# Block attention and feed-forward on one core: the mask rows ahead of the first splits, the weights' scalings behind the first casts, and shorter chains for the last query block

## The chip, the core and the metric

The kernel runs on one core of a Trainium2 chip. The metric is the time of one execution in microseconds (us). The engines named below are TensorE (PE; its weight loads are PEld), VectorE (DVE), ScalarE (ACT) and GpSimd (POOL); SP is the queue that issues the transfers (DMA) of this kernel.

## What is computed

The reference is block-causal attention over 8 batches of 8 heads, 576 positions and head size 64, followed by a feed-forward of two matrix products with a piecewise activation:

```python
scores = (1.0 / np.sqrt(64)) * np.matmul(q, k.transpose(0, 1, 3, 2))   # q, k, v: (8, 8, 576, 64)
mask = (pos[:, None] // 64) >= (pos[None, :] // 64)                    # pos = arange(576)
scores = np.where(mask, scores, -1000000000.0)
attn = np.exp(scores - np.max(scores, axis=-1, keepdims=True))
attn = attn / (np.sum(attn, axis=-1, keepdims=True) + 1e-09)
x = np.matmul(attn, v)              # then to (4608, 512)
h = x @ w_in                        # w_in: (512, 2048)
g = np.where(h >= 1, h, np.where(h <= -1, 0.0, (h + 1) ** 2 / 4))
return g @ w_out                    # w_out: (2048, 512)
```

## The kernel before

All matrix operands are kept as a sum of two parts, a rounded one and the rest, so that TensorE can take them in its fp32r type and the products come out near fp32: xh and xl for x, wih and wil for w_in, and the two halves of wo_split (in device memory) for w_out. `convert` splits 64 pieces of the weights (128x256 each): a load into bits on SP (L160), two scalings on ScalarE (L165, L166), three bit operations on VectorE (L167, L170, L173), an addition on GpSimd (L179), a cast on ScalarE (L181), a subtraction on GpSimd (L183).

Attention runs in 32 pairs of heads, four for each batch. Of a pair, queries and keys are loaded (qn, kn), split on VectorE (`split_q`, L310 and L311; `split_k`, L320 and L321), turned by TensorE through products with the identity (`turned`, L346), and cast on ScalarE into qb and kb (L351); the part that belongs in qa and ka is copied by VectorE for the first head of the first pair (L353) and by a transfer for all others (L357). The scores are two products, qa with ka (L391) and qb with kb (L394). qa and ka have four more partitions than the 64 of a head, which hold the rows that add the mask: they are made once in mrow, out of the selector sel (a tile msel with ones where the partition's number is that of the query tile), and moved into both heads' qa and ka by four transfers on SP (L148, L149). A softmax of a tile of 128 queries takes the negated maximum (L414), an exponential with a sum (L418), an addition of EPS and a reciprocal in `inverse` (L400, L401), and a scaling (L424).

The last blocks of 64 queries of both heads of a pair make one tile of their own in `scores_last`. Its 576 keys don't fit in one bank of PSUM (the matrix engine's result memory), so they come in two halves: two maxima (L438), their minimum after negation (L442), two exponentials with sums (L444), the sum of these (L448), `inverse`, the scaling (L450). After that TensorE turns the scaled rows, in `turn_last` (L463 in the first batches, L461 in the others, where they first move through a transfer, L239 or L246).

`attention_steps` is a generator with eight steps for each pair. The main loop draws after each of them as many weight pieces as are due (24 in the first 36 steps) and, from step 36 on, one step of the feed-forward: for 512 tokens, w_in (L646), the activation (L655 to L661), w_out (L670, L675). A scheduler sets each engine's order: the text of the program gives an instruction's place among equals, but it may move up when its inputs and slots are expected to be ready. `tc.issue_after(x)` keeps the instructions of the block behind x on x's engine. Tiles come from pools of few slots: a tile gets a slot when an earlier tile in it has been read for the last time. ident_f, mtmp and msel, and the bits of every second weight piece among the first 32, share the two slots of the tag t; the work tiles of those pieces share two slots of the tag gl.

## Time and profile before

| | |
|---|---|
| time, median of 3 runs | 1271.27 us (1271.11 to 1272.6) |
| the profiled execution | 1272.09 us, span of its instructions 1270.3 us |
| PE (matmuls) busy | 1210.7 us, 95% of the span |
| DVE busy | 856.4 us, 67% |
| ACT busy | 701.3 us, 55% |
| POOL busy | 456.3 us, 36% |

The shares are means over stages that differ: attention alone at the start, attention with feed-forward up to about 1075 us, feed-forward alone after that. So the busy times are read by stretches, and the first microseconds instruction by instruction. In the rows below an instruction has its start, its duration, its engine and line, the operation, result<-inputs with shapes, and in brackets how long the engine had been idle before it and what ended that. An instruction that waits inside its own execution shows a longer duration instead. Groups of instructions give a count, the busy time and the mean duration.

### The profile page before, as it was taken

Reading aid. Unit: us, or ns where it says so; the run is one execution under the profiler, and the core shown is the slowest. Engines: PE = TensorE matmul, PEld = TensorE weight load, DVE = VectorE, ACT = ScalarE, POOL = GpSimd, SP = SyncE. Lnnn points to the kernel's source line nnn. Section 1 sums busy time; section 2 is a strip of 40 time slices with the busy share of each in tenths; the row PEclk is TensorE's granted clock in tenths of the full one; section 3 lists DMA queues with packets and bytes.
Section 4 is the critical chain, followed back from the end, with each engine's and each line's share of the span. In section 5 each row is a group of like instructions: output and inputs, shape, how many; then the busy total and the mean of one; then the engine's idle time right before and its main releaser. Section 6 shows DMA issues by size and latency. Waiting matters only on the chain.

```text
span 1270.3 us, 20591 instructions
## 1 busy us (share of the span) xinstructions
PE 1210.7 (95%) x6496; PEld 1018.4 (80%) x6496; DVE 856.4 (67%) x2164; ACT 701.3 (55%) x1827; POOL 456.3 (36%) x454
## 2 busy tenths in 40 slices
PE   5879887899999999999999999999999999999998
PEld 4667666688888888888888888888888888888886
DVE  8998877857776777777777777777777676222222
ACT  5877656546565655566556656555565564222222
POOL 3555655523332333333333333333333332222222
PEclk9888989899999999999999999999999999999999
DMA  5656666655444545564455545454445443322432
GB/s 157 182 165 213 196 228 210 212 184 173 148 152 147 191 144 161 158 193 149 148 162 168 178 141 161 153 181 143 152 154 184 151 132 117 127 92 97 133 100 100
DMA packets 146093, 201.30 MB, mean 158 GB/s; under 512 B 63152, under 2 KB 93872, under 8 KB 145984
## 3 DMA queue, kind: packets, MB, share of 16 engines
q1 hardware_dynamic: 145984, 199.98, 50.4%
q8 instruction: 52, 0.85, 0.3%
q14 instruction: 57, 0.47, 0.1%
HBM read 120.59 MB, written 17.83 MB: 109 GB/s over the span
## 4 chain that ended last, share of the span: by engine, by line
PE 68%; DVE 8%; ACT 4%; issue 3%; DMA 3%; POOL 2%; SPq 0%; ACTq 0%; POOLq 0%; DVEq 0%
PE ph L646 26%; PE po L670 16%; PE po L675 8%; PE ps_av L500 7%; PE ps_t L461 3%; PE ps_s L394 3%; PE ps_s L391 3%; ACT pr L418 2%; PE ps_qk L346 2%; DMA prr<-pr 2%; DVE t L656 2%; DVE nm L414 1%; DVE t L659 1%; DVE pr L424 1%; POOL work L179 1%
## 5 line engine op out<-in xcount | busy, mean ns | idle before, releaser
L661 POOL TENSOR_TENSOR gl<-t,gh 128x512 fp32r<-128x512 f32 x144 | 186.9, 1298 | 604.7 <-ACT gh L660 301.8
L670 PE MATMUL po<-wo,gh 128*128 128x512 f32 x1152 | 296.9, 399 | 0.1
L656 DVE SCALAR_TENSOR_TENSOR t<-t 128x512 f32<-128x512 f32 x144 | 112.9, 784 | 200.2 <-ACT t L655 198.5
L646 PE MATMUL ph<-xh,wih 128*128 128x512 f32 x576 | 237.6, 413 | 2.7 <-DVE t L659 1.8
L670 PEld LDWEIGHTS po<-wo,gh 128*128 128x128 f32 x1152 | 207.7, 188 | 39.3 <-ACT gh L660 0.6
L646 PE MATMUL ph<-xl,wih 128*128 128x512 f32 x576 | 227.4, 395 | 0.9 <-DVE xl L536 0.9
L646 PE MATMUL ph<-xh,wil 128*128 128x512 f32 x576 | 227.4, 395 | 0.0
L655 ACT ACTIVATE t<-ph 128x512 f32<-128x512 f32 x144 | 86.1, 598 | 184.7 <-PE ph L646 184.7
L418 ACT ACTIVATE pr<-ps_s,nm 128x128 f32<-128x128 f32 (+3 forms) x256 | 134.4, 529 | 50.6 <-DVE nm L414 50.3
L414 DVE TENSOR_REDUCE nm<-ps_s 128x1 f32<-128x128 f32 (+3 forms) x256 | 123.6, 485 | 48.7 <-PE ps_s L394 47.4
L675 PE MATMUL po<-wo,gl 128*128 128x512 f32 x576 | 155.3, 391 | 0.0
L660 ACT CAST gh<-t 128x512 fp32r<-128x512 f32 x144 | 89.6, 622 | 102.1 <-DVE t L659 101.7
L391 PE MATMUL ps_s<-ka,qa 68*128 68x288 f32 (+4 forms) x384 | 122.5, 334 | 9.1 <-ACT kb L351 4.2
L646 PEld LDWEIGHTS ph<-xh,wil 128*128 128x128 f32 x576 | 109.1, 189 | 24.1
L675 PEld LDWEIGHTS po<-wo,gl 128*128 128x128 f32 x576 | 108.1, 188 | 23.3
L646 PEld LDWEIGHTS ph<-xh,wih 128*128 128x128 f32 x576 | 109.1, 189 | 21.7 <-DVE t L659 2.4
L646 PEld LDWEIGHTS ph<-xl,wih 128*128 128x128 f32 x576 | 109.6, 190 | 20.2 <-DVE xl L536 1.5
L394 PE MATMUL ps_s<-kb,qb 128*128 128x288 f32 (+4 forms) x384 | 121.4, 323 | 0.0
L454 ACT CAST pb<-ps_t 128x512 fp32r<-128x512 f32 (+1 forms) x120 | 65.5, 546 | 85.6 <-PE ps_t L461 83.8
L424 DVE TENSOR_SCALAR pr<-pr,sm 128x128 f32<-128x128 f32 (+3 forms) x256 | 104.8, 430 | 4.0
L336 POOL TENSOR_TENSOR vsr<-vn,vsr 64x64 fp32r<-64x64 f32 (+1 forms) x96 | 72.8, 768 | 88.6 <-ACT vsr L335 88.6
L456 DVE TENSOR_TENSOR pb<-ps_t,pb 128x512 fp32r<-128x512 f32 (+1 forms) x120 | 75.6, 630 | 40.4 <-ACT pb L454 39.9
(101 smaller groups left out, 1961.4 us busy)
## 6 DMA issues: line engine op xcount, KB each, us to landing
wo<-wo_split SPq DMA_DIRECT2D x144, 512.0 KB, 3.4
prr<-pr SPq DMA_DIRECT2D x96, 192.0 KB, 2.7
prr<-pr SPq DMA_DIRECT2D x72, 256.0 KB, 2.6
out_dram<-ob SPq DMA_DIRECT2D x36, 256.0 KB, 3.9
qn<-in_q_dram SPq DMA_DIRECT2D x32, 256.0 KB, 2.9
kn<-in_k_dram SPq DMA_DIRECT2D x32, 256.0 KB, 2.9
bits<-in_moe_w_in_dram SPq DMA_DIRECT2D x32, 256.0 KB, 3.6
bits<-in_moe_w_out_dram SPq DMA_DIRECT2D x32, 256.0 KB, 3.2
```

The costliest lines, as they stand in the source:

```text
L391: nc.tensor.matmul(ps, qa[:KA, j, c0 : c0 + P], ka[:KA, j, k0 : k0 + n], start=first, stop=False)
L394: nc.tensor.matmul(ps, qb[:, j, c0 : c0 + P], kb[:, j, k0 : k0 + n], start=False, stop=last)
L414: nc.vector.tensor_reduce(out=nm[:, i : i + 1], in_=ps[:, cs], axis=AX.X, op=ALU.max, negate=True)
L418: nc.scalar.activation(pr[:, cs], ps[:, cs], AF.Exp, bias=nm[:, i : i + 1], scale=1.0, accum_out=sm[:, i : i + 1],)
L424: nc.vector.tensor_scalar_mul(pr[:, cs], pr[:, cs], sm[:, i : i + 1])
L500: nc.tensor.matmul(ps[:, lo_col:], vt, x, start=first and i == 0 and m == 0, stop=last and i == len(parts) - 1 and m == len(mov) - 1,)
L646: nc.tensor.matmul(ph, w[:, cc, fs], x[:, cc, xs], start=(cc == 0 and i == 0), stop=(cc == NCC - 1 and i == 2),)
L656: nc.vector.scalar_tensor_tensor(out=t_, in0=t_, scalar=1.0, in1=t_, op0=ALU.min, op1=ALU.mult)
L660: nc.scalar.copy(gh, t_)
L661: nc.gpsimd.tensor_tensor(out=gl, in0=t_, in1=gh.bitcast(F32), op=ALU.subtract)
L670: nc.tensor.matmul(po[tt], gh[:, ts_], wo[:, w, :], start=(fc == 0 and w == 0), stop=False)
L675: nc.tensor.matmul(po[tt], gl[:, ts_], wo[:, 0, :], start=False, stop=fc == NFC - 1)
```

## The change

Four things are changed. msel gets a slot of the tag gl, is filled at the top of the function ahead of the identity, and by GpSimd alone. The zeroing of the last columns of qa and qb moves ahead of the mask rows, the four transfers of the mask rows directly behind them in the text, and both splits of the queries and keys (`split_queries` and `split_keys` hold the old bodies) stay behind the last mask row, by `issue_after(masked)`. The two scalings of a weight piece stay behind the last cast of turned queries of the first pair, by `issue_after(casts[-1])`. In `scores_last` the minimum becomes a tensor_scalar with one half's maximum as its scalar, and sum and EPS are added in one tensor_scalar, so that `inverse` isn't called there.

```diff
@@ -83,6 +83,13 @@
         return ps_w.tile([P, 512], F32, tag="work", name=name)
 
 
+    msel = ffn.tile([P, 512], F32, tag="gl", name="msel")
+    sel = msel[:NTL, : NTL * BLK].rearrange("p (t c) -> p t c", c=BLK)
+    nc.gpsimd.memset(msel[:NTL, : NTL * BLK], 0.0)
+    nc.gpsimd.affine_select(
+        out=sel, in_=sel, compare_op=ALU.not_equal, fill=1.0, base=0,
+        pattern=[[-1, NTL], [0, BLK]], channel_multiplier=1,
+    )
     ident_f = ffn.tile([P, 512], F32, tag="t", name="ident_f")[:, :P]
     make_identity(nc, ident_f)
     ident_r = const.tile([P, P], F32R, tag="ident", name="ident_r")
@@ -118,35 +125,27 @@
     vsr = [const.tile([P, NTL + 1, 2, D], F32R, tag=f"vsr{j}", name=f"vsr{j}") for j in range(2)]
 
     mtmp = ffn.tile([P, 512], F32, tag="t", name="mtmp")
-    msel = ffn.tile([P, 512], F32, tag="t", name="msel")
     nc.vector.memset(mtmp, 0.0)
-    nc.vector.memset(msel[:NTL], 0.0)
-    nc.gpsimd.affine_select(
-        out=msel[:NTL, : NTL * BLK].rearrange("p (t c) -> p t c", c=BLK),
-        in_=msel[:NTL, : NTL * BLK].rearrange("p (t c) -> p t c", c=BLK),
-        compare_op=ALU.not_equal, fill=1.0, base=0,
-        pattern=[[-1, NTL], [0, BLK]], channel_multiplier=1,
-    )
-    sel = msel[:NTL, : NTL * BLK].rearrange("p (t c) -> p t c", c=BLK)
+    for t_ in (qa, qb):
+        nc.vector.tensor_copy(
+            t_[:, :, SM:], mtmp[:, : 2 * (QW - SM)].rearrange("p (h c) -> p h c", h=2)
+        )
     for side in range(2):
         nc.vector.tensor_copy(mrow[:, side, :512], mtmp[:NTL, :512])
         nc.vector.tensor_copy(mrow[:, side, 512:S], mtmp[:NTL, : S - 512])
     rows = mrow[:, :, :SM].rearrange("p s (t c) -> p s t c", c=P)
     nc.vector.tensor_copy(rows[:, 0, :, :BLK], sel)
-    nc.vector.tensor_scalar_mul(rows[:, 1, :, BLK:], sel, MASKED)
-    for t_ in (qa, qb):
-        nc.vector.tensor_copy(
-            t_[:, :, SM:], mtmp[:, : 2 * (QW - SM)].rearrange("p (h c) -> p h c", h=2)
-        )
+    masked = nc.vector.tensor_scalar_mul(rows[:, 1, :, BLK:], sel, MASKED)
+    for j in range(2):
+        nc.sync.dma_start(qa[D:KA, j, :S].bitcast(F32), mrow[:, 0, :].bitcast(F32))
+        nc.sync.dma_start(ka[D:KA, j, :].bitcast(F32), mrow[:, 1, :].bitcast(F32))
     for t_ in pcs:
         nc.vector.tensor_copy(t_[BLK:], mtmp[BLK:, : 2 * BLK].rearrange("p (h c) -> p h c", h=2))
     for t_ in vsr:
         nc.vector.tensor_copy(
             t_[BLK:, NTL, :, :], mtmp[BLK:, : 2 * D].rearrange("p (h c) -> p h c", h=2)
         )
-    for j in range(2):
-        nc.sync.dma_start(qa[D:KA, j, :S].bitcast(F32), mrow[:, 0, :].bitcast(F32))
-        nc.sync.dma_start(ka[D:KA, j, :].bitcast(F32), mrow[:, 1, :].bitcast(F32))
+    casts = []
 
 
     def convert(n, source, hi, lo, done):
@@ -162,8 +161,10 @@
         low = bits[:, :, 0]
 
 
-        nc.scalar.mul(top, bits[:, :, 1].bitcast(F32), 2.0**-112)
-        nc.scalar.mul(low, low.bitcast(U32), 2.0**-29)
+
+        with tc.issue_after(casts[-1].ins):
+            nc.scalar.mul(top, bits[:, :, 1].bitcast(F32), 2.0**-112)
+            nc.scalar.mul(low, low.bitcast(U32), 2.0**-29)
         nc.vector.tensor_scalar(
             out=top, in0=top, scalar1=F32_TOP, scalar2=-F32_TOP, op0=ALU.min, op1=ALU.max
         )
@@ -304,6 +305,10 @@
 
         def split_q(self):
 
+            with tc.issue_after(masked.ins):
+                self.split_queries()
+
+        def split_queries(self):
             qn = self.nat.pop("q")[:, : 2 * NTL + 1, :]
             self.qs = att1.tile([P, 2 * NTL + 1, 2, D], F32R, tag="qs", name="qs")
             for c0, c1 in ((0, 2 * NTL), (2 * NTL, 2 * NTL + 1)):
@@ -314,6 +319,10 @@
             )
 
         def split_k(self):
+            with tc.issue_after(masked.ins):
+                self.split_keys()
+
+        def split_keys(self):
             kn = self.nat.pop("k")[:, : 2 * NTL + 1, :]
             self.ks = att1.tile([P, 2 * NTL + 1, 2, D], F32R, tag="ks", name="ks")
             for c0, c1 in ((0, 2 * NTL), (2 * NTL, 2 * NTL + 1)):
@@ -348,7 +357,9 @@
                 )
 
             turned = ps[:, :SM].rearrange("p (t c) -> p c t", t=NTL)
-            nc.scalar.copy(bt[:, j, :SM].rearrange("p (c t) -> p c t", t=NTL), turned)
+            cast = nc.scalar.copy(bt[:, j, :SM].rearrange("p (c t) -> p c t", t=NTL), turned)
+            if self.first and is_q:
+                casts.append(cast)
             if self.first and j == 0:
                 nc.vector.tensor_copy(
                     a[:D, j, :SM].rearrange("p (c t) -> p c t", t=NTL), turned[hi0 : hi0 + D]
@@ -439,14 +450,19 @@
                     out=nm[:, i : i + 1], in_=ps[:, :half], axis=AX.X, op=ALU.max, negate=True
                 )
                 banks.append(ps)
-            nc.vector.tensor_tensor(out=nm[:, 2:3], in0=nm[:, 0:1], in1=nm[:, 1:2], op=ALU.min)
+            nc.vector.tensor_scalar(
+                out=nm[:, 2:3], in0=nm[:, 0:1], scalar1=nm[:, 1:2], scalar2=None, op0=ALU.min
+            )
             for i in range(2):
                 nc.scalar.activation(
                     pr[:, i * half : (i + 1) * half], banks[i][:, :half], AF.Exp,
                     bias=nm[:, 2:3], scale=1.0, accum_out=sm[:, i : i + 1],
                 )
-            nc.vector.tensor_tensor(out=sm[:, 2:3], in0=sm[:, 0:1], in1=sm[:, 1:2], op=ALU.add)
-            self.inverse(sm[:, 2:3])
+            nc.vector.tensor_scalar(
+                out=sm[:, 2:3], in0=sm[:, 0:1], scalar1=sm[:, 1:2], scalar2=EPS,
+                op0=ALU.add, op1=ALU.add,
+            )
+            nc.vector.reciprocal(sm[:, 2:3], sm[:, 2:3])
             nc.vector.tensor_scalar_mul(pr, pr, sm[:, 2:3])
             self.pr["last"] = as_float32r(pr, self.plain) if self.hop else [pr]
 
```

The scheduler's orders for the two kernels differ on TensorE in about the first 960 matmuls, on the others there above all, and on VectorE also for each pair's last block. On ScalarE at the start of the program, before (L165 and L166 scale the first weight pieces, L351 casts turned queries and keys, L370 the last blocks):

```order
L165 ACT_TABLE_LOAD
L165 ACTIVATE work_202<-bits_201 128x256
L351 CAST qb_103<-ps_qk_150 128x512
L351 CAST kb_105<-ps_qk_157 128x512
L351 CAST qb_103<-ps_qk_164 128x512
L351 CAST kb_105<-ps_qk_187 128x512
L166 ACTIVATE bits_201<-bits_201 128x256
L370 CAST qb_103<-ps_qk_230 128x2x64
L165 ACTIVATE work_241<-bits_240 128x256
```

and with the change (the lines are now L360 for the casts, L166 and L167 for the scalings):

```order
L360 ACT_TABLE_LOAD
L360 CAST qb_108<-ps_qk_150 128x512
L360 CAST kb_110<-ps_qk_157 128x512
L360 CAST qb_108<-ps_qk_164 128x512
L360 CAST kb_110<-ps_qk_187 128x512
L166 ACTIVATE work_202<-bits_201 128x256
L167 ACTIVATE bits_201<-bits_201 128x256
L166 ACTIVATE work_212<-bits_211 128x256
L167 ACTIVATE bits_211<-bits_211 128x256
```

The four casts have gone ahead of the first scaling, and a second scaled piece ahead of the last blocks.

On SP at the start of the program, behind the loads of the first pair, before:

```order
L160 DMA bits_201<-in_moe_w_in_dram 128x512
L160 DMA bits_240<-in_moe_w_in_dram 128x512
L295 DMA qn_306<-in_q_dram 128x2x256
L148 DMA qa_102<-mrow_106 4x576
L149 DMA ka_104<-mrow_106 4x576
```

and with the change (L159 loads weights, L140 and L141 move the mask rows):

```order
L159 DMA bits_201<-in_moe_w_in_dram 128x512
L159 DMA bits_211<-in_moe_w_in_dram 128x512
L159 DMA bits_240<-in_moe_w_in_dram 128x512
L140 DMA qa_107<-mrow_111 4x576
L141 DMA ka_109<-mrow_111 4x576
```

The load of the second pair's queries has gone behind the mask rows, and a third load of weights has come ahead of them.

On VectorE, from behind the minimum of the second pair's last block (L442) to its scaling (L450), with sm_560 the block's sums, before (L167, L170 and L173 belong to weight pieces, L320 to the next pair's keys, L414 to maxima of other tiles):

```order
L170 TENSOR_SCALAR work_602<-work_602 128x256
L320 CAST ks_609<-kn_589 128x8x64
L173 SCALAR_TENSOR_TENSOR work_602<-work_602 128x256
L320 CAST ks_609<-kn_589 128x64
L414 TENSOR_REDUCE nm_615<-ps_s_613 128x1 x2
L448 TENSOR_TENSOR sm_560<-sm_560 128x1
L414 TENSOR_REDUCE nm_644<-ps_s_642 128x1
L400 TENSOR_SCALAR sm_560<-sm_560 128x1
L167 TENSOR_SCALAR work_673<-work_673 128x256
L401 RECIPROCAL sm_560<-sm_560 128x1
L167 TENSOR_SCALAR work_700<-work_700 128x256
L450 TENSOR_SCALAR pr_558<-pr_558,sm_560 128x576
```

and with the change, behind the minimum L453 (sm_559 the block's sums; L461 the sum, L465 the reciprocal, L466 the scaling; L168 and L174 weights, L425 maxima, L435 another tile's scaling):

```order
L435 TENSOR_SCALAR pr_531<-pr_531,sm_533 128x512
L425 TENSOR_REDUCE nm_613<-ps_s_611 128x1 x2
L174 SCALAR_TENSOR_TENSOR work_671<-work_671 128x256
L461 TENSOR_SCALAR sm_559<-sm_559 128x1
L425 TENSOR_REDUCE nm_642<-ps_s_640 128x1
L465 RECIPROCAL sm_559<-sm_559 128x1
L168 TENSOR_SCALAR work_698<-work_698 128x256
L466 TENSOR_SCALAR pr_557<-pr_557,sm_559 128x576
```

Between the sum and the scaling an addition and one bit operation on weights are gone; the keys' split and two bit operations have left the part ahead of the sum, and another tile's scaling has come in.

## Rows read from the trace of the kernel before

**Rows 1.** Busy time by stretches: us from:to, length, busy per engine (count), clock, DMA

```profile
12.00:100.00 88.00, 71.33 (x365) 57.97 (x365) 81.20 (x249) 69.92 (x215) 47.46 (x58) 0.88 0.60 176
...
100.00:300.00 200.00, 178.74 (x895) 142.13 (x895) 151.83 (x384) 123.24 (x345) 99.91 (x117) 0.96 0.65 206
...
300.00:1060.00 760.00, 754.46 (x4307) 647.91 (x4305) 553.13 (x1407) 451.33 (x1169) 259.25 (x233) 1.00 0.51 158
```

**Rows 2.** Timeline, start, DVE: start us, us, engine, line, operation, shapes [idle before <-releaser]

```profile
4.09 0.48 DVE L123 MEMSET msel<- 4x512 f32 x1
...
4.66 1.00 DVE L311 SCALAR_TENSOR_TENSOR qs<-qn,qs 128x576 fp32r<-128x576 f32 x1
...
6.39 0.20 DVE L320 CAST ks<-kn 128x64 fp32r<-128x64 f32 x1 [0.40 <-DMA kn<-in_k_dram]
...
6.62 0.76 DVE L321 TENSOR_TENSOR ks<-kn,ks 128x576 fp32r<-128x576 f32 x1
...
7.64 0.28 DVE L136 TENSOR_SCALAR mrow<-msel 4x256 fp32r<-4x256 f32 x1
```

**Rows 3.** The same timeline: PE, ACT and DVE up to the first scores

```profile
7.58 0.75 PE L346 MATMUL ps_qk<-ident_r,qs 128*128 128x128 f32 x4 [7.58 <-DVE ident_r L89]
...
10.26 0.43 ACT L165 ACTIVATE work<-bits 128x256 f32<-128x256 f32 x1 [8.25 <-DMA bits<-in_moe_w_in_dram]
...
10.72 0.29 DVE L167 TENSOR_SCALAR work<-work 128x256 f32<-128x256 f32 x1 [2.81 <-ACT work L165]
...
11.97 0.69 DVE L353 CAST ka<-ps_qk 64x512 fp32r<-64x512 f32 x1
...
12.02 0.61 ACT L351 CAST kb<-ps_qk 128x512 fp32r<-128x512 f32 x1
...
12.72 0.47 PE L391 MATMUL ps_s<-ka,qa 68*128 68x128 f32 x1 [2.62 <-DVE ka L353]
```

**Rows 4.** The same timeline: issues on the SP queue

```profile
6.66 1.06 SPq L160 DMA_DIRECT2D bits<-in_moe_w_in_dram  x2
...
9.17 0.61 SPq L149 DMA_DIRECT2D ka<-mrow  x1
```

**Rows 5.** DMA issues, 0 to 20 us: count, KB each, us to landing

```profile
qn<-in_q_dram SPq DMA_DIRECT2D x2, 256.0 KB, 3.9
...
kn<-in_k_dram SPq DMA_DIRECT2D x4, 16.0 KB, 2.5
```

**Rows 6.** Timeline, second pair: the last query block on DVE, and PE behind it

```profile
46.40 0.21 DVE L448 TENSOR_TENSOR sm<-sm 128x1 f32<-128x1 f32 x1
...
47.06 1.04 DVE L167 TENSOR_SCALAR work<-work 128x256 f32<-128x256 f32 x1
...
48.75 0.51 DVE L450 TENSOR_SCALAR pr<-pr,sm 128x576 f32<-128x576 f32 x1
...
49.41 1.30 PE L463 MATMUL ps_t<-ident_r,pr 128*128 128x128 f32 x5 [3.78 <-DVE sm L400]
```

**Rows 7.** Waits of PE, 0 to 100 us: us in total, times, longest

```profile
PE ps_t L463 <- DVE sm L400: 7.4, 3, 3.8
```

**Rows 8.** Groups by line, shape: count | busy us, mean ns | idle before

```profile
L400 DVE TENSOR_SCALAR sm<-sm 128x2 f32<-128x2 f32 x64 | 30.6, 478 | 26.1 <-ACT pr L418 26.1
...
L400 DVE TENSOR_SCALAR sm<-sm 128x1 f32<-128x1 f32 x160 | 23.1, 145 | 5.9 <-ACT pr L418 2.6
...
L442 DVE TENSOR_TENSOR nm<-nm 128x1 f32<-128x1 f32 x32 | 13.2, 412 | 0.9
...
L448 DVE TENSOR_TENSOR sm<-sm 128x1 f32<-128x1 f32 x32 | 5.9, 185 | 18.2 <-ACT pr L444 18.2
```

**Rows 9.** Timeline, GpSimd and DVE: a late minimum of a last query block

```profile
149.99 1.42 POOL L321 TENSOR_TENSOR ks<-kn,ks 128x576 fp32r<-128x576 f32 x1 [0.43 <-DVE ks L320]
...
150.31 1.12 DVE L442 TENSOR_TENSOR nm<-nm 128x1 f32<-128x1 f32 x1
```

**Rows 10.** Busy time by stretches, one of ten us

```profile
220.00:230.00 10.00, 7.40 (x19) 5.52 (x20) 8.12 (x25) 6.58 (x20) 4.92 (x6) 0.66 0.77 259
```

## The prediction

> **What bounds the kernel now.** I read the busy time by stretches first [rows 1]. From 300 us on TensorE works 754.5 of 760 us; what other engines save there has nowhere to go. From 12 to 100 us it works 71.3 of 88 and VectorE 81.2; from 100 to 300 us TensorE still idles 21.3 us. So time can be won before the first matmul, and where TensorE waits in the first 300 us. A head start gained there is kept, since the work after it is dense.
>
> The timeline of the start shows two waits. On VectorE the memset of msel stands at 4.09 us, between the splits, because its slot of the pool comes free only when mtmp has been read; the splits end at 7.38 (6.62 + 0.76), then comes the cast of the identity, and the last mask row is written at 7.64 to 7.92 [rows 2]. TensorE's first turn of queries waits for the identity until 7.58. On ScalarE the first weight scaling (L165) waits 8.25 us for its load, until 10.26, and the casts of the turned queries and keys (L351), whose turns were done from 8.3 on, queue behind it. VectorE stands 2.81 us before L167, which takes ScalarE's result; its cast into ka ends at 12.66 and the first scores start at 12.72 [rows 3].
>
> In the second pair the last query block shows the other kind: its sum at 46.40, its scaling at 48.75 to 49.26, and TensorE, whose next work turns that block, stands still for 3.78 us [rows 6]. Three such waits make 7.4 us of the first 100 [rows 7].
>
> **The change part by part: the start.** In the changed order the mask rows and the identity's cast stand ahead of the splits, the memset of msel is on GpSimd. VectorE's work up to the splits' end loses 0.48 (memset) and keeps the rest: ident_r, L135, L136 only change places, some 0.8 us (0.28 for L136, the others alike) going ahead of the query split. That split is then done some 0.6 us later than it was (0.8 less what VectorE had stood idle before it); the key split ends at the same 7.4 us, since it waits for the last piece of kn, landed at 6.39. The query split would end at 5.66 + 0.6, and the query turns start right behind it, at about 6.3 us instead of 7.58 [rows 2]; the key turns start at 7.4 instead of 8.1. All turns are done some 0.7 us earlier.
>
> ScalarE now has the four casts first. Each takes about 0.6 us, as the last of the four in [rows 3]; the first key cast ends near 8.8, the copy into ka near 9.5 instead of 12.66. So the casts are 3 us earlier, but **what is late next** is the mask rows' transfer into qa and ka, which the first scores read. SP is the queue to look at: it issues in order, and the mask rows stand behind two weight loads (1.06 us for both) and one query load and the one into ka is issued from 9.17 to 9.78 [rows 4]. The new order has three weight loads and no query load ahead of them: 256 KB as well, and no more than 0.6 us to issue, so the same place within 0.1 us, and the same issue times. Having the rows ready at 4 us instead of 7.9 thus buys nearly nothing. The ka row then lands, from its issue near 9.2: after 2.5 us if like the 16 KB loads, after 3.9 if like the 256 KB loads of queries [rows 5], so at 11.7 or 13.1; for less there is only that issue starts are 0.6 us apart, so no earlier than 9.8. I take 11.6, nearest to the small loads (9 KB here). The first scores start there instead of at 12.72: 1.1 us earlier, with bounds of 2.9 earlier and 0.4 later.
>
> Of this VectorE has to make use, as it is nearly full from 12 us on. Its 2.81 us in front of L167 stay open up to 10.7, as L165 still waits for its load to land at 10.26 [rows 3]. The two L353 copies (0.7 us each) now fill this gap, but VectorE then waits for the first scores instead. I count **1.0 us** for the start, with bounds of -0.4 and 2.4 (for more than 2.4, VectorE would have to have no idle time at all there).
>
> **The small operations.** Per pair one VectorE instruction goes: sum, add of EPS and reciprocal become two instead of three. The row of the single add is 145 ns [rows 8], the step to the next instruction some 0.2 us by my estimate. In nine pairs up to 300 us that is 1.8 us of VectorE's chain in front of the last block's scaling.
>
> Further, the order of what lies between changes. In the second pair, between the sum (46.40) and the scaling (48.75) there stand two L167 of weights, one of which took 1.04 us; in the new order one of them is left there. TensorE waits for just this chain (3.78 us) [rows 6]. So this wait shrinks by 0.2 (only the add) up to 1.2 us (the long L167 too). The first pair's order loses one L167 from the same place, so the same bounds; for the third to fifth I take 0.2 each. That is 1.0 to 3.0 us for five pairs; moved work has to be done elsewhere on a full VectorE, so I take **2.0**.
>
> The minimum (L442) has a mean of 412 ns for one number per partition; L400 on the same width has 145, on two numbers 478 [rows 8]. One of 1.12 us began and ended inside a subtraction of GpSimd, the end of both being 151.4 [rows 9]. The new form, a tensor_scalar of width one, is that of L400's 145 ns row. From 100 to 300 us such waits are worth 1.0 (rows 9) and at most 32 x 0.04 = 1.3 in L448 (185 ns against 145 [rows 8]); most of L442's others come after 300 us, where TensorE is full. With the 0.8 us of four shorter chains in these 200 us the bounds are 0 and 3.1. I take **0.7**, nearer to nothing, since TensorE is idle there only a tenth of the time [rows 1].
>
> The Trainium skill speaks against this last term at one point. "VectorE: DVE Perf Modes", section on mode 2x_2P, lets a one-source operation in SBUF use both read ports when its outermost non-unit dimension is even, or odd and equal for source and destination, and "SBUF — State Buffer", section "two separate sides", says such an operation and GpSimd shut each other out for a whole instruction. If width one counts as odd and equal, the new minimum would wait as the old one did, this term would be 0.3 instead of 0.7, and the sum 3.3 instead of 3.7 us. The two rows of L400 speak otherwise, 478 ns at width two and 145 at width one [rows 8], so I keep 3.7.
>
> **Rivals.** *The full engine keeps it.* VectorE stays the bound up to 100 us, and only the VectorE time that is gone comes back: 0.48 of memset and five adds, 1.0, together 1.5 us; the shorter waits of TensorE are filled by moved weight work. For it: 81.2 of 88 us [rows 1]. Against it: the 6.8 us in which VectorE stands idle in the same stretch, so it isn't the bound throughout. That gives 1271.3 - 1.5 = 1269.8.
>
> *A new order costs the clock.* TensorE's order differs in about the first 960 matmuls (transposes and scores swap places with the first feed-forward matmuls). Where TensorE has waited, stretches at the lower of its clock levels (1.2 of 2.4 GHz) follow: 220 to 230 us has 7.40 us of work and a granted clock of 0.66 [rows 10], against 1.00 from 300 us on [rows 1]. One further stretch like this costs 0.34 x 10 = 3.4 us if TensorE is the bound behind it. Its place is the stretch from 100 to 300 us; it opens if a wait of TensorE there grows to that of the second pair, 3.78 us. With the first rival's 1.5 us it gives 1271.3 - 1.5 + 3.4 = 1273.2, slower. A stretch avoided, by the same row, would give 1264.2 together with my sum.
>
> *The mask rows don't come earlier.* If they land at 13.1, as a load of 256 KB would, the start loses 0.4 instead of winning 1.0: 3.7 - 1.4 = 2.3 us, 1269.0. For it: three weight loads ahead of them on SP. Against it: 9 KB, and a start at 12.72 that was a cast's doing.
>
> **How the numbers follow.** 1.0 + 2.0 + 0.7 = 3.7 us. The profiled execution took 1272.1 us (span 1270.3), 0.8 above the median of 1271.3: it would take 1268.4, and the median 1267.6. Chances: this sum 0.52, the first rival 0.2, the mask rows' 0.12, the clock rival 0.16. What a measurement here can tell from no change is 0.2%, 2.5 us: faster than 1268.7 or slower than 1273.8. Of the sum's case I count 0.43 as faster and 0.09 (its lower terms) as the same; the first rival and the mask rows' give 0.07 to faster and 0.25 to the same, the clock rival 0.06 to the same and 0.10 to slower. So 0.50 faster, 0.40 same, 0.10 slower. Range: 1264.2 (a clock stretch less) to 1272.9, most of the clock rival's side left out.
>
> **What would show it.** First scores near 11.6 us with the wait in front of them put down to the mask rows' transfer, not to a cast; ScalarE's first four instructions being casts that end near 10 us. The wait of TensorE before the second pair's last block under 3.0 us. The new minimum at about 0.15 us through the whole run. Matmul lines in the dense part unchanged. If the stretches up to 300 us show more time at the lower clock, the second rival is right; if TensorE's idle time up to 100 us stays while VectorE's busy time falls by 1.5 us only, the first.

## The result: 0.24% slower, and the profile after

The changed kernel takes 1274.61 us in the median of 9 runs, beside 1271.27 us of the kernel before on the same chip: ratio 1.0024, 95% interval 1.0014 to 1.0035, so 3.1 us slower (1.8 to 4.4). The forecast was 3.7 us faster. The profiled execution took 1274.26 us (span 1272.5). Further down the kernel before was run anew beside each group of kernels (medians from 1269.8 to 1271.3), and each ratio is to those runs.

Busy time by stretches in the changed kernel, columns as in [rows 1], with two stretches of ten us:

```profile
12.00:100.00 88.00, 71.84 (x381) 58.14 (x382) 79.44 (x249) 70.18 (x217) 48.10 (x60) 0.94 0.61 179
100.00:300.00 200.00, 176.45 (x861) 140.09 (x860) 155.48 (x372) 119.22 (x332) 98.58 (x114) 0.92 0.63 202
300.00:1060.00 760.00, 753.42 (x4305) 646.72 (x4304) 544.52 (x1378) 451.13 (x1166) 259.24 (x235) 1.00 0.51 158
110.00:120.00 10.00, 6.63 (x28) 5.11 (x28) 6.65 (x19) 6.93 (x20) 2.90 (x4) 0.59 0.57 187
...
130.00:140.00 10.00, 6.30 (x24) 4.57 (x24) 8.99 (x19) 7.50 (x23) 7.36 (x9) 0.76 0.60 174
```

Beside [rows 1]: up to 100 us VectorE is busy 1.8 us less, TensorE idles about as long as before (16.2 us, was 16.7), and its granted clock is higher (0.94, was 0.88). From 100 to 300 us TensorE idles 23.6 us (was 21.3) and the granted clock is 0.92 (was 0.96). The dense part is unchanged. As a measure of a stage I use below what TensorE loses in it: its idle time plus busy time x (1 - granted clock). From 100 to 300 us that is 23.6 + 14.1 = 37.7, before 21.3 + 7.1 = 28.4. The measure is rough, as the mean clock of a stretch also counts the time at the lower level in which TensorE has nothing to do.

The minima of the last query blocks show when it happens (starts on VectorE, of pairs 1 to 6, 8 and 20; after less before): +0.6, +2.2, +0.5, -1.8, -2.8, **+2.9**, +2.2, +2.7 us. This execution was behind in the first three pairs and ahead in the fourth and fifth; from the fifth pair's minimum to the sixth's it lost 5.7 us.

The start, in the timeline of the changed kernel:

```profile
9.39 0.60 ACT L360 CAST kb<-ps_qk 128x512 fp32r<-128x512 f32 x1
...
9.15 0.61 SPq L141 DMA_DIRECT2D ka<-mrow  x1
...
10.52 0.29 DVE L168 TENSOR_SCALAR work<-work 128x256 f32<-128x256 f32 x1 [0.78 <-ACT work L166]
...
12.12 0.45 PE L402 MATMUL ps_s<-ka,qa 68*128 68x128 f32 x1 [2.58 <-DMA ka<-mrow]
...
13.35 0.62 DVE L425 TENSOR_REDUCE nm<-ps_s 128x1 f32<-128x128 f32 x2 [2.21 <-PE ps_s L405]
...
18.46 0.69 DVE L425 TENSOR_REDUCE nm<-ps_s 128x1 f32<-128x512 f32 x1
...
22.93 1.09 PE L479 MATMUL ps_t<-ident_r,pr 128*128 128x128 f32 x4 [2.48 <-DVE nm L453]
```

The casts end at 9.99 and the first scores wait for the mask rows, as forecast; but these land 3.0 us after the start of their issue (2.4 taken; 2.5 to 2.8 in the other kernels with the same issue time), so the first scores start 0.6 us earlier than in [rows 3]. VectorE gains nothing from that. From 8 us to its first maximum it stands idle 0.56 and 0.21 us before its two copies (L364), 0.78 before the first weight piece and 2.21 before the maximum, 3.8 us together; in the kernel before it was 2.81 us [rows 3] and 0.33 us, 3.1 together. From 8 to 112 us the sum of its idle time is 11.1 us, before 10.9.

Then the order of the first pair takes the lead of the scores back: the maximum of the tile of 512 keys, whose scores are done early, stands behind other tiles' scalings and a weight piece. In the kernel before it ran 2.7 us sooner:

```profile
13.97 1.20 DVE L414 TENSOR_REDUCE nm<-ps_s 128x1 f32<-128x128 f32 x3 [0.33 <-PE ps_s L394]
...
15.73 0.69 DVE L414 TENSOR_REDUCE nm<-ps_s 128x1 f32<-128x512 f32 x1
```

TensorE waits 2.48 us to turn that tile (the profile names L453, which stands on VectorE right behind the tile's scaling), and the first pair's last block is 0.6 us late.

In the second pair the one long wait of [rows 6] has become four (TensorE's timeline of the changed kernel):

```profile
43.39 0.40 PE L402 MATMUL ps_s<-ka,qa 68*128 68x288 f32 x1 [1.09 <-DVE ka L382]
...
45.42 0.54 PE L355 MATMUL ps_qk<-ident_r,qs 128*128 128x128 f32 x4 [0.43 <-DVE xl L552]
...
47.69 0.66 PE L479 MATMUL ps_t<-ident_r,pr 128*128 128x128 f32 x4 [1.20 <-DVE pr L435]
...
50.13 1.30 PE L479 MATMUL ps_t<-ident_r,pr 128*128 128x128 f32 x5 [1.20 <-DVE sm L411]
```

Together they make 3.9 us. The wait in front of the last block is 1.20 us where it was 3.78, but the block is turned 0.72 us later than before (49.41).

### The profile page after: what moved, and what is told of

It is laid out like the page before. It is cut to its first block, busy times and chain, and to the rows that moved or that the text cites. A ratio compares the mean times of both kernels' runs of the same rounds, so it can differ in the third digit from the quotient of the medians.

```text
span 1272.5 us, 20569 instructions
## 1 busy us (share of the span) xinstructions
PE 1211.6 (95%) x6496; PEld 1018.4 (80%) x6496; DVE 852.8 (67%) x2131; ACT 701.5 (55%) x1827; POOL 458.0 (36%) x455
## 4 chain that ended last, share of the span: by engine, by line
PE 68%; DVE 15%; ACT 6%; DMA 4%; issue 4%; POOL 2%; SPq 0%; ACTq 0%; POOLq 0%; DVEq 0%
PE ph L662 26%; PE po L686 16%; PE po L691 8%; PE ps_av L516 7%; PE ps_t L477 3%; PE ps_s L402 3%; PE ps_s L405 3%; PE ps_qk L355 3%; DMA prr<-pr 2%; DVE pr L435 2%; ACT pr L429 2%; DVE nm L425 2%; DVE t L672 2%; DVE t L675 1%; POOL work L180 1%
## 5 line engine op out<-in xcount | busy, mean ns | idle before, releaser
L671 ACT ACTIVATE t<-ph 128x512 f32<-128x512 f32 x144 | 86.0, 597 | 188.9 <-PE ph L662 188.8
L425 DVE TENSOR_REDUCE nm<-ps_s 128x1 f32<-128x128 f32 (+3 forms) x256 | 123.4, 484 | 48.9 <-PE ps_s L405 47.4
L435 DVE TENSOR_SCALAR pr<-pr,sm 128x128 f32<-128x128 f32 (+3 forms) x256 | 107.3, 440 | 3.9
```

Of the source, the lines that this page charges most:

```text
L425: nc.vector.tensor_reduce(out=nm[:, i : i + 1], in_=ps[:, cs], axis=AX.X, op=ALU.max, negate=True)
L435: nc.vector.tensor_scalar_mul(pr[:, cs], pr[:, cs], sm[:, i : i + 1])
```

## Where the 5.7 us go: one place of TensorE's order

At the fifth pair the feed-forward begins. In the kernel before, the last products of TensorE's first step of it (L646) stand ahead of the fifth pair's turns, ScalarE's Relu (L655) follows at once, and the second step's twelve products fill the time that the transfer of the next scores (prs) takes. Timeline before:

```profile
108.56 0.39 PE L646 MATMUL ph<-xh,wil 128*128 128x512 f32 x1
...
108.99 0.60 ACT L655 ACTIVATE t<-ph 128x512 f32<-128x512 f32 x1 [2.11 <-PE ph L646]
...
113.07 0.80 PE L646 MATMUL ph<-xh,wih 128*128 128x512 f32 x1 [1.75 <-DVE t L659]
...
117.66 0.45 PE L461 MATMUL ps_t<-ident_r,prs 128*128 128x128 f32 x4
```

In the changed order the last two products of the first step come behind the turns, so the Relu (L671) comes behind the exponentials, the second step can't begin, and the turn of prs stands ahead of it with nothing to cover its transfer. Timeline after:

```profile
108.52 0.63 PE L662 MATMUL ph<-xh,wil 128*128 128x512 f32 x1
...
110.31 0.50 SPq L240 DMA_DIRECT2D prs<-pr  x1
...
111.64 0.62 ACT L671 ACTIVATE t<-ph 128x512 f32<-128x512 f32 x1
...
112.76 0.72 PE L477 MATMUL ps_t<-ident_r,prs 128*128 128x128 f32 x4 [3.61 <-DMA prs<-pr]
...
114.86 0.80 PE L662 MATMUL ph<-xh,wih 128*128 128x512 f32 x1 [0.61 <-DVE t L675]
...
135.96 0.69 PE L402 MATMUL ps_s<-ka,qa 68*128 68x384 f32 x1 [2.79 <-ACT kb L360]
```

Two waits of TensorE, 3.61 and 2.79 us, and in the stretch of each more of the lower of the clock's two levels (1.2 of 2.4 GHz): 0.59 granted from 110 to 120 us, 0.76 from 130 to 140 (before 0.83 and 1.00). From 108 to 160 us, which takes in the whole of the first wait (busy time by stretches, before and after):

```profile
108.00:160.00 52.00, 44.43 (x225) 34.72 (x225) 44.14 (x108) 34.88 (x100) 30.21 (x36) 0.97 0.66 205
```

```profile
108.00:160.00 52.00, 43.15 (x199) 33.32 (x197) 44.94 (x106) 32.58 (x92) 29.60 (x34) 0.84 0.60 191
```

TensorE's loss is 7.6 + 1.3 = 8.9 us before and 8.9 + 6.9 = 15.8 after: of the difference 1.3 us is idle time and 5.6 clock.

## First experiments: the parts, and a hold

**Each part alone.** The small operations (only `scores_last` changed), the new start (everything else), the casts alone (only `issue_after(casts[-1].ins)` on the scalings of weights).

> The kernel before with the new scores_last alone. TensorE's order around the turn of the fifth pair comes out as in the changed kernel. Theory A: the loss of 4 to 5.7 us is here too, against up to 2 us won by shorter chains: 1273 to 1275 us. Theory B (the new start costs): faster, 1268.5 to 1270. Theory C (the small operations' new form costs by itself): 1274 or more, and the minima of pairs in the dense part each a little later.

1279.39 us, ratio 1.0068 (1.0055 to 1.0081).

> The changed kernel with the old scores_last: the new start alone (mask rows, splits behind them, scalings of weights behind the casts). TensorE's order has the turn of the fifth pair ahead of part of its cover, as in the changed kernel. Theory A: 1273 to 1275. Theory B: 1274 or more, with the loss seen before 100 us. Theory C: 1270 to 1271, the 0.6 us of the start won.

1280.29 us, ratio 1.0068 (1.0054 to 1.0082).

> The kernel before with one edit: the scalings of weights stay behind the first casts of turned queries. Mask rows, splits and scores_last are as before. TensorE's order around the turn of the fifth pair is as in the kernel before. Theory A: no loss at 110 us; the start wins some tenths, 1270 to 1271.3. Theory B: if the casts are what costs, 1273 or more; if the mask rows, 1271. Theory C: 1271.

1271.44 us, ratio 0.9995 (0.9981 to 1.0009).

Each half of the change loses more by itself than both together, which the parts' own work can't explain. The two that lose have the new order at the fifth pair, the one that doesn't has the old. Theory A's 1273 to 1275 is too low for both halves; B fits only the new start and C only the small operations.

**The turn put back.** Only the turn of prs is held behind the second step:

```diff
-                nc.tensor.matmul(
+                mm = nc.tensor.matmul(
                     ph, w[:, cc, fs], x[:, cc, xs],
...
+        if c == 0 and fc == 1:
+            for x in held:                     # fifth pair's turn(0, 2)
+                tc.add_manual_dep(x.ins, mm.ins.name, ...)
```

> The changed kernel with one place of TensorE's order put back: the four products that turn the tile of queries with 512 keys of the fifth pair (L477) stay behind the twelve w_in products of the second ffn step (L662), as in the kernel before. Theory A (the loss is made at this place: the turn stands ahead of its cover, waits 3.6 us for its transfer, and the lower clock follows): of the 5.7 us lost between 109 and 153 us most is won back; about 1269.5 us (1268.5 to 1271), faster than before by 0.1% or more. Theory B (the new start costs): nothing comes back, 1274.5. Theory C (the new form of the small operations costs): 1274.5 too.

1272.51 us, ratio 1.0011 (1.0002 to 1.0020): less is won back than theory A expected. TensorE's timeline says why: the wait has moved to the products that were to be the cover, since the Relu still comes late.

```profile
117.17 0.80 PE L667 MATMUL ph<-xh,wih 128*128 128x512 f32 x1 [5.91 <-DVE t L689]
```

That points to the first step's last two products as the root, not to the turn. The next runs move these.

## The place by itself: pushed and held

**Push**: the kernel before, with the first of those two products held behind the turns of the next pair's queries. The rest of the text is as before, and the scheduler does the rest: in the trace TensorE's order leaves that of before at the 421st matmul, and from there on it differs from the changed kernel's in 16 places. **Two holds**: fifth pair's `turn(0, 0)` behind `ffn_in(0, 0)`, `turn(0, 2)` behind `ffn_in(0, 1)`, in the changed kernel and in its two halves.

```diff
# push, in ffn_in of the kernel before
+                if c == 0 and fc == 0 and cc == NCC - 1 and i == 1:
+                    tc.add_manual_dep(mm.ins, held[-1].ins.name, ...)
# two holds, in ffn_in; held = {0: turn(0, 0)'s, 1: turn(0, 2)'s transposes of the fifth pair}
+        for x in held.get(fc, ()) if c == 0 else ():
+            tc.add_manual_dep(x.ins, mm.ins.name, ...)
```

> The kernel before with one thing added: of the first feed-forward step's twelve w_in products (L646), the second of the last three stays behind the turns of the sixth pair's queries. TensorE's order then is as before up to there and as in the changed kernel from there on, the turn of the fifth pair's tile of 512 keys ahead of its cover included. Start and scores_last are as before. Theory A2 (the order at this place makes the loss: the first step's activation comes behind the exponentials, so the second step's products can't cover the transfer, and TensorE waits twice and runs at the lower clock): 1274.5 to 1278 us, with a wait of 3 us or more near 113 us and one of 2 us or more near 136. Theory D (any order here costs the same; the loss comes with what each edit does to the other engines): 1271 to 1272.

1278.71 us, ratio 1.0068 (1.0052 to 1.0085). One edge costs 8 us. The minima of the first five pairs start within 1 us of those of the kernel before, the sixth 8.5 us later, the last 8.1. Its waits, in TensorE's timeline, and its stretch:

```profile
115.00 0.72 PE L461 MATMUL ps_t<-ident_r,prs 128*128 128x128 f32 x4 [2.80 <-ACT pb L454]
...
138.88 0.44 PE L391 MATMUL ps_s<-ka,qa 68*128 68x384 f32 x1 [2.07 <-ACT kb L351]
```

```profile
108.00:160.00 52.00, 42.81 (x195) 33.37 (x195) 41.32 (x102) 30.98 (x87) 30.87 (x37) 0.84 0.61 194
```

> The changed kernel with the order at that place put back by two holds on the fifth pair: the turn of its tiles of 128 and 256 keys stays behind the first feed-forward step's w_in products, and the turn of the tile of 512 keys behind those of the second step. ScalarE's and VectorE's orders around the first activation come out as in the kernel before. Theory A2: 1268.5 to 1270.5, the loss of 4 to 6 us gone, the lead of 2 us or so at 110 us kept. Theory D: 1273 to 1275.

1271.69 us, ratio 1.0010 (0.9999 to 1.0021).

> The kernel before with the new scores_last and the same two holds. Theory A2: 6 to 8 us less than without the holds (1279.4), so 1271 to 1273. Theory D: 1278 to 1280.

1271.56 us, ratio 1.0007 (0.9995 to 1.0019).

> The changed kernel with the old scores_last and the same two holds. Theory A2: 5 to 8 us less than without the holds (1280.3), so 1272 to 1275. Theory D: 1279 to 1281.

1272.05 us, ratio 1.0013 (0.9999 to 1.0027).

TensorE's loss from 108 to 160 us, from the same rows of each kernel (idle + clock, us; one execution each):

| kernel | old order at the place | new order |
|---|---|---|
| before / push | 7.6 + 1.3 = 8.9 | 9.2 + 6.8 = 16.0 |
| small operations, with / without holds | 7.1 + 3.1 = 10.2 | 8.8 + 5.6 = 14.4 |
| new start, with / without holds | 9.0 + 1.3 = 10.3 | 9.7 + 6.8 = 16.5 |
| changed, with / without holds | 7.9 + 3.1 = 11.0 | 8.9 + 6.9 = 15.8 |

The place makes the loss: pushed into the kernel before it costs 8 us, held in the two halves it gives back 7.8 and 8.2. In the changed kernel it costs 5 us by the table, but only 1 to 3 by the times; why the times show less there isn't settled. With the place held nothing is faster than before either: the changed kernel stands between theory A2's 1268.5 to 1270.5 and theory D. The forecast gain is missing too.

## Where the gain is

Four more kernels, all with the two holds at the fifth pair: the changed one with the first pair's scalings held behind the maximum of 512 keys; that, and SP's weight loads behind the mask rows; the mask rows and splits alone; the casts with the small operations.

```diff
# in scores of the first pair; top: the maximum of 512 keys, early: the scalings of its other tiles
+                for x in early:
+                    tc.add_manual_dep(x.ins, top.ins.name, ...)
# in convert; moved: the last transfer of the mask rows
+        with tc.issue_after(moved.ins):
             nc.sync.dma_start(bits, ...)
```

> The changed kernel with the two holds at the fifth pair (1271.7 us) and a third one: in the first pair the scalings of the tiles of 384 and 384 keys stay behind the maximum of the tile of 512 keys on VectorE, as in the kernel before. Theory E (the head start of the first scores is lost in the first pair, by VectorE's order, and would be kept from there on): the first pair's minimum starts some 1 us ahead of the kernel before instead of 0.8 us behind it, and the time falls by 1 to 2 us, to 1269.7 to 1270.7. Theory F (time won in the first 100 us is given back in the next 200, as VectorE has the same work to do and TensorE waits elsewhere): the first pair is early, and the time stays within 0.7 us of 1271.7.

1273.20 us, ratio 1.0018 (1.0006 to 1.0030). The first pair's minimum came 0.6 us ahead of before as wanted, and the second pair's was 0.2 us behind it.

> As the kernel with three holds, and on SP the weight loads stay behind the four transfers of the mask rows, which are so issued some 2 us earlier. First scores near 10.2 us instead of 12.1. Theory E: 1.5 to 2 us less than with the three holds alone, 1267.5 to 1269. Theory F: the same as that kernel within 0.7 us, about 1271.

1271.35 us, ratio 1.0005 (0.9994 to 1.0017). First scores at 11.43, not 10.2: with the weight loads gone the next pair's query loads (three issues, 1.7 us) moved ahead of the mask rows on SP.

> The kernel before with the mask rows and the splits as changed, the weights' scalings and scores_last as before, and the two holds at the fifth pair. The maximum of the tile of 512 keys stands early on VectorE here. Theory E: 1269.5 to 1270.7. Theory F: 1270.6 to 1272.

1275.02 us, ratio 1.0040 (1.0025 to 1.0054).

> The kernel before with the scalings of weights behind the first casts, the new scores_last and the two holds at the fifth pair; mask rows and splits as before. Theory E: the half microsecond of the casts and up to 2 us of the shorter chains, 1268.5 to 1270. Theory F: 1270 to 1271.5, no different from the kernel before.

1272.80 us, ratio 1.0022 (1.0011 to 1.0033).

Theory E fails in all four. Theory F's times hold for the second; the other three are slower than either theory said, and what costs them wasn't taken apart (of the mask rows and splits alone, TensorE loses 31.5 us from 12 to 112 us, before 26.3). No way of starting earlier showed a gain. Is anything won before 100 us kept? One run makes the start late, one takes VectorE's work away:

```diff
# late, in attention_steps of the kernel before
...
+        for _ in range(11):
+            pause = nc.vector.memset(slow[:, :G1], 0.0)
+        with tc.issue_after(pause.ins):
+            first.split_q()
+            first.split_k()
# no clamp, in convert; with the two holds
+        if n >= 24:
             nc.vector.tensor_scalar(out=top, in0=top, scalar1=F32_TOP, ...)
```

> The kernel before with eleven memsets of 128x320 on VectorE in front of the first splits: the first pair starts some 3 us later, and from the 138th matmul on TensorE's order is word for word that of the kernel before. Theory G (a shift of the start is kept to the end, as the work behind it is dense): the time rises by as much as the first scores move, 2 to 3 us, to about 1273.5. Theory F (the stages up to 300 us take such a shift up, or give it back, by other waits and the clock): it stays within 1 us of the kernel before.

1272.74 us, ratio 1.0016 (0.9999 to 1.0033), with the first scores 1.2 us late, less than meant. It is in line with a shift that is kept, but too small to tell.

> The kernel before with the two holds at the fifth pair (which alone change nothing in its order), leaving out the clamp (L167) of the first 24 weight pieces, so their large values aren't limited: 24 VectorE instructions of 0.28 us or more, 6.7 us of its work in the first 110 us. Theory H (VectorE's work bounds the first 110 us, and what is won there is kept): 5 to 7 us earlier at the fifth pair's minimum, and about 1265 us. Theory F: 2 to 6 us earlier at the fifth pair, and less than 2 us of it left at the end, 1269 to 1271.

1275.76 us, ratio 1.0045 (1.0028 to 1.0061): less work and 5.7 us slower. Both theories fail. Its order is new again, and the place at the fifth pair is held, so other places cost too (from 12 to 112 us TensorE loses 2 us more than before, from 160 to 300 us 3 more).

**The order held.** So the order of all five queues was frozen to the kernel before's over the first 1200 matmuls (some 320 us), by a table of places at the end of the program. In the traces of the first and third run below, TensorE, ScalarE and GpSimd have before's order throughout:

```diff
+    for engine, places in order.items():       # of before, by place in the text
+        row = [traced[engine][p] for p in places]
+        for one, two in zip(row, row[1:]):
+            tc.add_manual_dep(two, one.name, ...)
```

> The kernel before with the new scores_last, and with the order of all five queues held to the order of before over the first 1200 matmuls (some 320 us) by a table of places; only the minimum's form changes and the add of EPS is gone. Theory I (the edit is worth what it takes out, and only the new order had eaten it): 0.7 to 2.5 us faster than before, 1268 to 1270. Theory F (what is won in the first 110 us is given back up to 300 us in any order): within 0.6 us of before.

1270.57 us, ratio 1.0002 (0.9991 to 1.0014): no gain is shown, as theory F says.

> The changed kernel with its own order in the first pair, and from the 46th to the 1200th matmul the order of before on all five queues by a table of places. Theory I: 1 to 3.7 us faster than before, the sum of the prediction or part of it, 1267 to 1269.5. Theory F: within 0.6 us of before; either way some 3 us less than the changed kernel in its own order.

1271.55 us, ratio 1.0009 (0.9998 to 1.0020): some 2 us of the 3.1 us lost went with the order behind the first pair, and in the old order there is no gain either.

> The kernel before leaving out the clamp (L167) of the first 24 weight pieces, so their large values aren't limited, with the order of all five queues held to the order of before over the first 1200 matmuls. Theory I: VectorE's 6.7 us less work in the first 110 us show, 3 us or more faster than before, 1264 to 1268. Theory F: within 1 us of before, 1269.5 to 1271.5.

1263.90 us, ratio 0.9946 (0.9928 to 0.9965).

Without the clamps the kernel takes 12 us less in before's order than in the scheduler's own (with the two holds). In the held order 24 clamps are worth 6.9 us (4.4 to 9.1). At the step of an undisturbed one, 0.2 us from its start to the next one's, they take 4.8 us of VectorE; as they ran in the kernel before, with the waits inside them, 9.9 us. The gain lies between the two, and it is kept: the minima of this execution stand 7.1 us ahead of those of the kernel before at the fifth pair and 8.1 us ahead at the last. So time taken off VectorE in the first 110 us reaches the end, in the held order. Leaving out the clamps also shortens the chain of each weight piece; this run doesn't tell the two apart, the next version does in part. Up to 112 us (before, then this kernel):

```profile
12.00:112.00 100.00, 81.84 (x422) 66.06 (x422) 91.97 (x283) 78.61 (x241) 54.19 (x67) 0.90 0.61 178
```

```profile
12.00:112.00 100.00, 82.88 (x444) 66.29 (x445) 92.06 (x277) 83.24 (x256) 56.19 (x70) 0.97 0.63 192
```

VectorE is as busy as before and 22 more matmuls are done, as one expects if VectorE bounds this stage; TensorE's loss falls from 18.2 + 8.2 to 17.1 + 2.5 us. The small operations, in the same held order, bring nothing, since they take nothing off VectorE. Groups of DVE from 12 to 112 us, before and after (count, busy us, mean ns):

```profile
L400 DVE TENSOR_SCALAR sm<-sm 128x1 f32<-128x1 f32 x22 | 3.1, 142 | 0.5 <-ACT pr L418 0.5
...
L442 DVE TENSOR_TENSOR nm<-nm 128x1 f32<-128x1 f32 x5 | 0.7, 146 | 0.0
...
L448 DVE TENSOR_TENSOR sm<-sm 128x1 f32<-128x1 f32 x4 | 0.6, 162 | 0.0
```

```profile
L461 DVE TENSOR_SCALAR sm<-sm 128x1 f32<-128x1 f32 x5 | 1.0, 202 | 0.0
...
L453 DVE TENSOR_SCALAR nm<-nm 128x1 f32<-128x1 f32 x5 | 1.0, 198 | 0.0
```

By these durations minimum, sum and EPS took 146 + 162 + 142 = 450 ns a pair, and now 198 + 202 = 400: 0.25 us over five pairs. But VectorE starts its next instruction before such a short one has ended (timeline of the second pair, before and after):

```profile
44.25 0.15 DVE L442 TENSOR_TENSOR nm<-nm 128x1 f32<-128x1 f32 x1
44.32 0.29 DVE L170 TENSOR_SCALAR work<-work 128x256 uint32<-128x256 uint32 x1
```

```profile
46.48 0.20 DVE L453 TENSOR_SCALAR nm<-nm 128x1 f32<-128x1 f32 x1
46.60 1.04 DVE L435 TENSOR_SCALAR pr<-pr,sm 128x512 f32<-128x512 f32 x1
```

From a start to the next one, where the next had nothing to wait for, it is 65 + 84 + 60 = 209 ns on average from 12 to 112 us, and now 120 + 123 = 243. Counted that way nothing is saved.

**A version that beats both.** If VectorE's time is the price, work should go to ScalarE, in the held order:

```diff
# turned_last and split_q (the other branches left out); early: the first five pairs
+                if self.early:
+                    nc.scalar.copy(last_blocks(a)[:D], blocks[hi0 : hi0 + D])
...
+                if self.early and not self.first:
+                    nc.scalar.mul(self.qs[:, c0:c1, 0, :], qn[:, c0:c1, :], SCALE)
```

> The kernel before with VectorE's casts of the last blocks into qa and ka (L371) of the first five pairs and its scalings of the queries (L310) of the second to fifth pair on ScalarE, and the order of all five queues held to that of before over the first 1200 matmuls, the moved ones at the same places. Nothing is left out of the computation. VectorE has ten casts of 0.28 us and four scalings of 0.42 and 0.12 us less, some 5 us up to 112 us. Theory I (VectorE's time in this stage reaches the end one for one): 3 to 5 us faster than before, 1265.5 to 1267.5. Rival K (ScalarE, which works 70 of 88 us there, hands its own 6 us on to the exponentials that VectorE waits for): within 1.5 us of before, or slower.

1267.79 us, ratio 0.9981 (0.9970 to 0.9991): 2.4 us faster than before (1.1 to 3.8), about half of the 5 us taken off VectorE by their durations. Theory I's 3 to 5 us and rival K's 1.5 both miss it. Its stretch shows ScalarE's share risen from 78.6 to 85.9 of 100 us:

```profile
12.00:112.00 100.00, 80.62 (x435) 65.02 (x435) 90.97 (x276) 85.92 (x269) 55.13 (x69) 0.97 0.62 187
```

So the rule holds in part. That ScalarE hands some of the rest on is likely but wasn't taken apart.

## Why the prediction was wrong, step by step

- **The start, 1.0 us.** The casts, the mask rows and SP's part came as described, 0.6 us earlier instead of 1.1 for the scores. VectorE "then waits for the first scores instead", as the prediction says; the step that failed is to count 1.0 us all the same. Its idle time only moved (3.8 us up to the first maximum, 3.1 before), and the new order put the maximum of 512 keys 2.7 us late. In eight kernels with the new mask rows and casts the scores started 0.6 to 1.3 us earlier than in [rows 3], and none of them was faster than before; e3_pin3, with that maximum put ahead again, wasn't either.
- **The small operations, 2.0 + 0.7 us.** Priced at the wait of TensorE that they shorten. The wait did shrink (3.78 to 1.20), below the 3.0 named; others in the same seven microseconds took it up. With the order held the edit measured 0.3 us slower (1.1 faster to 1.8 slower). The mis-sized terms are the step of 0.2 us that a dropped addition was to save, which is 60 ns, and the new operation's duration, 200 ns where 145 was taken.
- **The minimum's lock with GpSimd.** The reading of the rows was right: all 32 new minima take 195 to 216 ns, 29 of them beside an instruction of GpSimd, and none is held up as L442 was (412 on average). Of the Trainium skill's page "VectorE: DVE Perf Modes" (mode 2x_2P), the reading by which width one would count as odd and equal is not borne out here. The two-wide L411 takes 153 to 164 ns where GpSimd does nothing and 567 on average where it starts inside an instruction of GpSimd. The lock's end is worth nothing: 23 of the 32 minima stand after 300 us, where TensorE is full.
- **The full engine (first rival, 0.2).** Right that the shorter waits of TensorE would not come back: its idle time up to 100 us stayed, while VectorE was busy 1.8 us less. The 1.5 us that it left as a gain showed in no run; with the order of before behind the first pair (e5_after_frozen) the change is 1.1 us slower (0.3 faster to 2.5 slower).
- **A new order costs the clock (second rival, 0.16).** Right as to the loss, with its place (100 to 300 us), its point (a wait of some 3.8 us; 3.61) and its kind; its price of 3.4 us was low (5.6 us of clock from 108 to 160 us, by the rough measure). The failed step is the chance: I saw that some 960 matmuls had a new order and still summed the parts as if the order stayed. The order was the larger term throughout, from 0 to 8 us at one place.
- **The mask rows (third rival).** They landed at 12.1, between the two values. Against this rival the prediction held that the start at 12.72 was a cast's doing. Some 0.4 us of it was: in two kernels with the old start (e1_small and push) the first scores wait for the mask rows, until 12.25 and 12.31, so a second wait stood right behind that for the cast.

## What to carry to other kernels

Where a scheduler sets the order, an edit has two effects, its own and that of the order it causes; look for the first places where two orders differ, ask of each turn, transfer and activation there what covered it before, and try the edit with the order held before judging it. Shortening a wait of one engine need not pay as long as another engine is full: count the full engine's time, and count it from one start to the next, not by durations. And longer waits can cost more through the clock behind them than by themselves: here 1.3 us more idle time went with 5.6 us more of loss by the clock.

## What the runs showed that I had not expected

- A one-wide VectorE operation with a constant takes 143 ns (L411), with a number out of a tile as its scalar 212 (L453, L461); from its start to the next one it is 64 and some 120 ns up to 112 us. All of the changed kernel:

```profile
L411 DVE TENSOR_SCALAR sm<-sm 128x1 f32<-128x1 f32 x128 | 18.3, 143 | 6.9 <-ACT pr L429 4.9
L461 DVE TENSOR_SCALAR sm<-sm 128x1 f32<-128x1 f32 x32 | 6.8, 212 | 14.1 <-ACT pr L457 14.1
L453 DVE TENSOR_SCALAR nm<-nm 128x1 f32<-128x1 f32 x32 | 6.8, 212 | 1.0
```

- One execution's lead early on says little. The changed kernel, the one with the turn put back and the one with two holds have the same order on every queue up to the fifth pair, and their minima there stand at -2.8, -0.4 and +1.4 us from before's. A stretch of one profile is evidence for a place, not for a microsecond.
